# Banks of PSUM in a fused attention and mixer kernel: three for transposes and second products, three for the product groups

## The chip, the cores and the metric

One core of a Trainium2 chip runs the whole program. The metric is the device time of one execution in microseconds (us). Three executions of the kernel before were timed, and one more was taken by the profiler.

## The reference

Attention over 4 batches, 8 heads, 576 positions and head size 64, with a mask: the first four heads see only the last 32 positions (local), the other four only positions of the same residue modulo 32 (strided). Behind it stand two feed-forward blocks in fp32:

```python
scores = np.where(masks[None, :, :, :], scale * np.matmul(q, k.transpose(0, 1, 3, 2)), -1e9)
attn = np.exp(scores - np.max(scores, axis=-1, keepdims=True))
attn = attn / (np.sum(attn, axis=-1, keepdims=True) + 1e-09)
x = np.matmul(attn, v)                              # heads side by side: (4, 576, 512)
h = gelu(x @ w_in); u, v = h[..., :512], h[..., 512:]
v_n = (v - mean(v)) / sqrt(var(v) + 1e-6) * g_ln
v_s = np.einsum('ts,bsd->btd', w_sg, v_n) + b_sg[None, :, None]
x = x + (u * v_s) @ w_out                           # the mixer
xn = (x - mean(x)) / sqrt(var(x) + 1e-6) * g_2
out = x + np.maximum(xn @ w_ch1, 0.0) @ w_ch2       # the last stage
```

## The kernel before, in words

Every fp32 product of the mixer is made of three matmuls on high and low halves (`mm3`, lines 247 to 249). The mixer runs over the four batches, and in each over four segments of product groups: v (five tiles of 128 positions and 512 columns, `v_mm`, lines 598 to 610), u (eight groups of 12 matmuls of 288 columns, `u_group`), g (eight groups of 14, `sg_group`) and y (eight groups of 12, `y_group`). A group fills one bank of PSUM, and the bank is free again when ScalarE (ACT) or VectorE (DVE) has read it: a gelu for v and u (line 354), a product into `z` for g (line 687), an addition into `y` for y (line 717). Of v's fifth tile the two halves are added first (lines 617 and 618). What follows a v tile is `v_norm`: mean and variance on DVE, a power on GpSimd (POOL, line 635), and the scaled tile `vn` on ACT (line 638) and DVE (line 641). Only two buffers `g2` hold the gelus of v, so the gelu of tile t waits for the last reader of tile t - 2. All groups of g need `vn` of all five tiles.

Between the groups stands the attention of the next batch, four pairs of heads, two local (nine blocks of 64 queries) and two strided. A pair has scores (`attn_s`, on PE with masks and maxima on DVE), exponentials (`attn_e`, ACT) and `attn2`: the weights are transposed on PE (`attn_turn`, line 515), copied out of PSUM, multiplied by the values (`attn_values`, lines 542 and 559) and copied into `x32`. In the names, `ps_t` is a bank of transposes, `ps_pv` one of second products, `ps_sc` one of scores.

PSUM has eight banks, in three pools for the whole program:

```python
ps_s = pool("ps_s", 2, space=PSUM)
ps_a = pool("ps_a", 2, space=PSUM)
ps_d = pool("ps_d", 4, space=PSUM)
```

`ps_s` holds scores, `ps_a` transposes and second products, `ps_d` the groups of v, u, g and y. A local pair takes three banks' worth of transposes (four, four and one block) and two of second products (five and four blocks), a strided one two and two.

The start, which is attention of batch 0 and the first four v tiles, runs in an order written out by hand (`START`). These four v tiles are accumulated side by side in the four banks of `ps_d`; the fifth follows when the first has had its gelu. From there on the order on each engine is made by a scheduler out of the program's order and the hooks (`hook(b, segment, group, function)`: called ahead of that group). The hooks of batch 0 at the first u group load the last quarter of `w_in`, and the spatial weights `wsg` are loaded from the fourth u group on (`WSG_AT`), but the scheduler takes both far forward. An engine works its own queue in order. The last stage (`last_stage`) uses all eight banks, and its products are `ps_p` and `ps_m`.

Of the kernel before, what the change touches and what calls it, by code (L numbers as in the profile page):

```python
# [12 lines left out]
F32 = mybir.dt.float32  # L13
# [5 lines left out]
PSUM = bass.MemoryType.PSUM  # L19
# [5 lines left out]
P = 128  # L25
# [160 lines left out]
def mixer_kernel(ctx: ExitStack, tc: tile.TileContext, io, out):  # L186
# [9 lines left out]
    def pool(name, bufs=1, **kw):  # L196
        guard = tc.tile_pool(name=name, bufs=bufs, **kw)
        pools[name] = guard
        return guard.__enter__()

    def close(*names):
        for n in names:
            pools.pop(n).__exit__(None, None, None)
# [4 lines that stand above are left out]
# [284 lines left out]
        attn_sum(b, p)  # L492
        attn_norm(b, p)

    pTs = {}

    def attn_turn(b, p):
        p3 = pend.pop((b, p))[0]
        local = p < NP // 2
        ntr = NLB if local else (NSG + 1) // 2  # L500
        c = P
        pT = pTs[b, p] = at.tile([P, ntr * c], F32, tag=f"pT{local}", name="pT", bufs=1)
        kr = LW if local else P
        for t0 in range(0, ntr, 4):
            m = min(4, ntr - t0)
            ps = ps_a.tile([P, 512], F32, tag="a", name="ps_t")
            rows = kr
            for t in range(t0, t0 + m):
                if local:
                    src = p3[:, t, :]  # L510
                else:
                    e = min(2 * t + 2, NSG)
                    src = pts[p % 2][:, 2 * t * SLOT:e * SLOT]
                    rows = (e - 2 * t) * SLOT
                nc.tensor.transpose(ps[:rows, (t - t0) * c:(t - t0 + 1) * c], src, ident)  # L515

            def copy(r, t, e):
                if t < e:
                    o, i = pT[:r, t * c:e * c], ps[:r, (t - t0) * c:(e - t0) * c]
                    if p in PT_DVE[min(b, 1)]:  # L520
                        nc.vector.tensor_copy(o, i)
                    else:
                        nc.scalar.activation(o, i, AF.Copy)

            copy(kr, t0, t0 + m - (rows < kr))
            if rows < kr:
                copy(rows, t0 + m - 1, t0 + m)

    def attn_values(b, p):
        pT, vt = pTs.pop((b, p)), vts.pop((b, p))  # L530
        local = p < NP // 2
        if p == 0:
            x32s[b] = dw.tile([P, NP, S], F32, tag="x32", name="x32", bufs=2)
            xhls[b] = win.tile([P, 2, NP, SX], F32R, tag="xhl", name="xhl")
        x32 = x32s[b]
        if local:
            for b0 in range(0, NLB, 5):
                m = min(5, NLB - b0)
                ps = ps_a.tile([P, 512], F32, tag="a", name="ps_pv")
                for i in range(b0, b0 + m):  # L540
                    for h in range(2):
                        nc.tensor.matmul(
                            ps[64 * h:64 * h + 64, (i - b0) * QB:(i - b0 + 1) * QB],
                            lhsT=vt[:LW, (i * 2 + h) * D:(i * 2 + h + 1) * D],
                            rhs=pT[:LW, i * P + 64 * (h ^ (i % 2)):i * P + 64 * (h ^ (i % 2)) + QB],
                            start=True, stop=True)
                if p in X32_DVE[min(b, 1)]:
                    nc.vector.tensor_copy(x32[:, p, b0 * QB:(b0 + m) * QB], ps[:, :m * QB])
                else:
                    nc.scalar.activation(x32[:, p, b0 * QB:(b0 + m) * QB], ps[:, :m * QB], AF.Copy)  # L550
        else:
            x3 = x32[:, p, :].rearrange("p (a r) -> p r a", r=STRIDE)
            for o in range(2):
                ps = ps_a.tile([P, 512], F32, tag="a", name="ps_pv")
                ks = slice(64 * o, 64 * o + 64)
                m = (NSG + 1 - o) // 2
                for j in range(m):
                    for h in range(2):
                        nc.tensor.matmul(
                            ps[64 * h:64 * h + 64, j * GW:(j + 1) * GW],  # L560
                            lhsT=vt[ks, (j * 2 + h) * D:(j * 2 + h + 1) * D],
                            rhs=pT[ks, j * P + 64 * (h ^ o):j * P + 64 * (h ^ o) + GW],
                            start=True, stop=True)
                full = m if o else m - 1
                nc.scalar.activation(
                    x32[:, p, :].rearrange("p (a r) -> p a r", r=STRIDE)[:, :, :30]
                    .rearrange("p a (j s) -> p j s a", s=2 * RG)[:, :, o * RG:(o + 1) * RG, :],
                    ps[:, :full * GW].rearrange("p (j r a) -> p j r a", r=RG, a=NPOS), AF.Copy)
                if full < m:
                    r0 = 2 * full * RG  # L570
                    nc.scalar.activation(
                        x3[:, r0:STRIDE, :],
                        ps[:, full * GW:full * GW + (STRIDE - r0) * NPOS].rearrange("p (r a) -> p r a", a=NPOS),
                        AF.Copy)
# [17 lines left out]
    def attn2(b, p):  # L592
        for step in (attn_turn, attn_values, attn_high, attn_low, attn_copy):
            step(b, p)
# [176 lines left out]
    def flush():  # L771
        while late_lows:
            late_lows.pop(0)()
# [42 lines left out]
    def keep(i):  # L816
        nc.sync.dma_start(out=w1_d[i], in_=w1[i].rearrange("p n a f -> p (n a f)").bitcast(F32))
# [44 lines left out]
    def prepare(n):  # L862
        for fn, a in units[done[0]:done[0] + n]:
            if fn is piece and a[1] < 2 and late_lows and wseq.index(a) in PRE:
                flush()
            fn(*a)
        done[0] += n
        if FLUSH:
            flush()
# [557 lines left out]
    def on(fn):  # L1427
        return lambda p: fn(0, p)

    first = {"q": on(attn_load), "m": on(attn_load_v), "K": on(attn_banks), "S": on(attn_scores),  # L1430
             "M": on(attn_max), "E": on(attn_exp), "U": on(attn_sum), "N": on(attn_norm), "T": on(attn_turn),
             "V": on(attn_values), "H": on(attn_high), "L": on(attn_low), "C": on(attn_copy), "w": load_w_v,
             "a": convert_w_v, "b": split_w_v, "v": v_part, "f": fill, "y": fetch_w_u,
             "c": lambda i: load_consts() if i == 0 else nc.sync.dma_start(out=g_v, in_=io["g_v"])}
# [7 lines left out]
    def hook(b, seg, i, fn, *args):  # L1442
        hooks.setdefault((b, seg, i), []).append((fn, args))
# [12 lines left out]
    def right(name, bufs=1):  # L1456
        big[name] = pool("r_" + "_".join(map(str, name)) if isinstance(name, tuple) else name, bufs, side="right",
                         reuse_waits="tile")
        order_r.append(big[name])

    order_r = []

    def open_a():
        close("at")
        right("wst")
        right("nm")
        right("sr")
        right("rb")
        big["norm", 0] = big["nm"].tile([P, KD * TC + 2 * TH], F32, tag="n0", name="n0")
        big["stg"] = big["wst"].tile([P, 3072], U32, tag="stg", name="stg")  # L1470
        big["stg2"] = big["wst"].tile([P, 1792], U32, tag="stg2", name="stg2")
# [13 lines left out]
    def open_d():  # L1485
        close("dn", "dw", "cw")
        for i in (1, 2):
            right(("w2p", i))
        right(("w2", NW - 1))
        right("h")  # L1490
        right("tmp")
        right("ev")
        right("lt")
        right("yc")
        big["late", 0] = big["nm"].tile([P, NLATE, TH], F32, tag="n0", name="late")
        big["late", 1] = big["lt"].tile([P, NF - NLATE, TH], F32, tag="lt", name="late2")

    last = B - 1
    hook(last, "v", 0, open_a)
    hook(last, "g", 0, open_b)  # L1500
    hook(last, "y", 0, open_c)
# [12 lines left out]
    def run(b, seg, n, fn):  # L1514
        for i in range(n):
            for h, args in hooks.get((b, seg, i), ()):
                h(*args)
            fn(b, i)
# [5 lines left out]
    for b, seg in order:  # L1524
        n, fn = segs[seg]
        run(b, seg, n, v_post0 if (b, seg) == (0, "v") else fn)
    open_d()
    prepare(max(0, 13 - done[0]))
    keep(1)
    last_stage()  # L1530
# [17 lines left out]
```

## Time and profile before

| what | us |
|---|---|
| median of the three timed runs | 666.51 |
| the three runs | 666.35, 666.51, 2217.13 |
| the profiled execution | 667.92 |
| its span, first to last instruction | 666.0 |
| PE busy in the span | 648.0 |
| DVE, ACT, POOL busy | 521.7, 397.9, 19.3 |

The profiled execution is 1.9 us longer than its span, and 1.4 us above the median of the timed runs. Matmuls are pipelined: a row's duration runs from issue to a modelled end, so two rows overlap, and the pace is the distance of their starts. A bracket at a row's end is the idle time of the engine ahead of it and what ended it. The mixer takes the first 300 us or so, the last stage the rest.

### The profile page before, as it was taken

To read this page: it belongs to the slowest core of one execution; us is meant where nothing else is said; L and a number is where in the kernel's file an instruction comes from. 1 tells how busy PE (TensorE), PEld (TensorE's weight loads), DVE (VectorE), ACT (ScalarE), POOL (GpSimd) and SP (SyncE) were. 2 spreads that over 40 slices of the span, in tenths; PEclk is the share of its full clock that TensorE was granted. 3 is DMA by queue.
4 is the path that set the end of the run, shared out by engine and by line. 5 is a ranking of instruction groups with operands and counts; after the bars stand their busy time and mean duration, and the time that the engine had idled before them with its cause. 6 is when DMAs were issued, how large, how long until landed. Compare 5 with 4: busy or idle time off the path is not lost.

```text
span 666.0 us, 12893 instructions
## 1 busy us (share of the span) xinstructions
PE 648.0 (97%) x4958; PEld 618.6 (93%) x4958; DVE 521.7 (78%) x997; ACT 397.9 (60%) x908; POOL 19.3 (3%) x24
## 2 busy tenths in 40 slices
PE   8989999999999998999999999999999999999997
PEld 6778989989897988999999999999999999999997
DVE  5979888586668688997799898558474776799993
ACT  4878967284458546645567965357663544766440
POOL 0011011000110001000000000000000000000000
PEclk9999999999999999999999999999999999999999
DMA  7793333458443470429997716499900879522234
GB/s 252 261 299 88 120 108 127 136 168 248 134 140 98 159 224 26 174 96 328 334 348 290 275 56 216 145 324 313 314 5 0 256 244 361 169 78 64 70 101 130
DMA packets 58444, 121.21 MB, mean 182 GB/s; under 512 B 4944, under 2 KB 28112, under 8 KB 57360
## 3 DMA queue, kind: packets, MB, share of 16 engines
q1 hardware_dynamic: 58384, 120.40, 54.2%
q8 instruction: 39, 0.64, 0.4%
q14 instruction: 21, 0.17, 0.1%
HBM read 87.35 MB, written 33.03 MB: 181 GB/s over the span
## 4 chain that ended last, share of the span: by engine, by line
PE 79%; DMA 6%; ACT 6%; DVE 6%; issue 2%; POOL 1%; SPq 0%; ACTq 0%; POOLq 0%; DVEq 0%
PE ps_p L994 26%; PE ps_m L1217 17%; PE ps_o L247 3%; PE ps_o L249 3%; PE ps_o L248 3%; PE ps_y L249 2%; PE ps_y L247 2%; PE ps_y L248 2%; DMA w_scratch<-w_p 2%; PE ps_g L247 2%; PE ps_g L248 2%; PE ps_g L249 2%; DMA stg<-in_w_ch 2%; PE ps_t L515 1%; PE ps_u L247 1%
## 5 line engine op out<-in xcount | busy, mean ns | idle before, releaser
L994 PE MATMUL ps_p<-x,w 128*128 128x384 f32 x1008 | 182.8, 336 | 0.8 <-ACT u L1187 0.5
L994 PEld LDWEIGHTS ps_p<-x,w 128*128 128x128 f32 x1008 | 174.2, 188 | 4.8 <-ACT u L1187 2.0
L1217 PE MATMUL ps_m<-t,w2c 128*128 128x384 f32 x420 | 74.3, 334 | 0.0
L1217 PEld LDWEIGHTS ps_m<-t,w2c 128*128 128x128 f32 x420 | 72.9, 188 | 0.0
L247 PE MATMUL ps_u<-xhl,winl 128*128 128x288 f32 x128 | 38.1, 297 | 1.6 <-ACT u L354 1.6
L247 PE MATMUL ps_g<-wsg,vn 128*128 128x288 f32 x128 | 39.0, 305 | 0.0
L249 PE MATMUL ps_g<-wsg,vn 128*128 128x288 f32 x128 | 38.3, 299 | 0.0
L248 PE MATMUL ps_g<-wsg,vn 128*128 128x288 f32 x128 | 38.1, 297 | 0.0
L249 PE MATMUL ps_y<-gt,wout 128*128 128x288 f32 x128 | 37.8, 296 | 0.0
L249 PE MATMUL ps_u<-xhl,winh 128*128 128x288 f32 x128 | 37.7, 295 | 0.0
L248 PE MATMUL ps_u<-xhl,winh 128*128 128x288 f32 x128 | 37.7, 294 | 0.0
L247 PE MATMUL ps_y<-gt,wout 128*128 128x288 f32 x128 | 37.6, 296 | 0.0
L248 PE MATMUL ps_y<-gt,wout 128*128 128x288 f32 x128 | 37.5, 294 | 0.0
L249 PE MATMUL ps_o<-h,w2x 128*128 128x384 f32 x96 | 32.1, 334 | 0.0
L248 PE MATMUL ps_o<-h,w2x 128*128 128x384 f32 x96 | 32.1, 334 | 0.0
L247 PEld LDWEIGHTS ps_u<-xhl,winl 128*128 128x128 f32 x128 | 24.0, 188 | 2.5 <-ACT u L354 2.1
L635 POOL TENSOR_TENSOR rs<-ve,neghalf 128x1 f32<-128x1 f32 x20 | 19.1, 958 | 242.3 <-DVE ve L633 242.3
L247 PEld LDWEIGHTS ps_g<-wsg,vn 128*128 128x128 f32 x128 | 24.1, 188 | 0.6
L717 DVE TENSOR_TENSOR y<-ps_y,x 128x288 f32<-128x288 f32 x32 | 14.4, 453 | 12.8 <-PE ps_y L249 12.0
L249 PEld LDWEIGHTS ps_g<-wsg,vn 128*128 128x128 f32 x128 | 24.0, 188 | 0.2
L248 PEld LDWEIGHTS ps_g<-wsg,vn 128*128 128x128 f32 x128 | 24.0, 188 | 0.1
L248 PEld LDWEIGHTS ps_u<-xhl,winh 128*128 128x128 f32 x128 | 24.0, 188 | 0.2
(344 smaller groups left out, 1631.3 us busy)
## 6 DMA issues: line engine op xcount, KB each, us to landing
w_scratch<-w SPq DMA_DIRECT2D x8, 1792.0 KB, 7.0
w<-w_scratch SPq DMA_DIRECT2D x24, 512.0 KB, 5.1
stg<-in_w_ch SPq DMA_DIRECT2D x22, 512.0 KB, 5.5
w<-w_scratch SPq DMA_DIRECT2D x36, 256.0 KB, 4.6
raw_p<-in_w_ch SPq DMA_DIRECT2D x20, 256.0 KB, 3.1
blk<-w_scratch SPq DMA_DIRECT2D x10, 512.0 KB, 5.4
qk<-in_qk_s SPq DMA_DIRECT2D x8, 601.0 KB, 4.3
qk<-in_qk_l SPq DMA_DIRECT2D x8, 592.0 KB, 5.0
```

The source lines that it names most:

```text
L247: nc.tensor.matmul(ps, lhsT=ll, rhs=rh, start=first, stop=False)
L248: nc.tensor.matmul(ps, lhsT=lh, rhs=rl, start=False, stop=False)
L249: last_mm[0] = nc.tensor.matmul(ps, lhsT=lh, rhs=rh, start=False, stop=last)
L515: nc.tensor.transpose(ps[:rows, (t - t0) * c:(t - t0 + 1) * c], src, ident)
L635: nc.gpsimd.tensor_tensor(out=rs, in0=ve, in1=neghalf[:, :1], op=ALU.pow)
L717: nc.vector.tensor_tensor(out=y[:, cs], in0=o, in1=x32[:, d, cs], op=ALU.add)
L994: nc.tensor.matmul(o, lhsT=w[:, n0 + nk * k, a, :], rhs=x[:, c, k, :], start=first and k == 0 and n == 0, stop=k == 1 and n == 2, skip_gro ...
L1217: nc.tensor.matmul(banks[e, half][:, :TH], lhsT=sl[m, e][a][:, i, :], rhs=g[:, c, half * TH:(half + 1) * TH], skip_group_check=True, start ...
```

## The change

From the first u group of batch 0 to the last y group of batch 3, the pools are three banks for `ps_a` and three for `ps_d`. Both pools are closed and opened again at that group (a hook), and once more, back to two and four, ahead of the last stage. A tile of a reopened pool waits for what last used its bank. In a local pair the second bank of second products (blocks five to eight) is no tile of its own any more: it lies in columns 128 on of the bank that holds the transpose of the ninth block. This holds for the start too.

```diff
@@ attn_turn
-    pTs = {}
+    pTs, shared = {}, {}
...
             ps = ps_a.tile([P, 512], F32, tag="a", name="ps_t")
+            if local and t0 == 8:
+                shared[b, p] = ps[:, P:]
@@ attn_values
-                ps = ps_a.tile([P, 512], F32, tag="a", name="ps_pv")
+                ps = shared.pop((b, p)) if b0 else ps_a.tile([P, 512], F32, tag="a", name="ps_pv")
@@ behind the hooks of the mixer
+    def banks(a, d):
+        nonlocal ps_a, ps_d
+        close("ps_d", "ps_a")
+        ps_a = pool("ps_a", a, space=PSUM, reuse_waits="tile")
+        ps_d = pool("ps_d", d, space=PSUM, reuse_waits="tile")
+
+    hook(0, "u", 0, banks, 3, 3)
@@ ahead of the last stage
     open_d()
+    banks(2, 4)
```

The scheduler makes another order of it. On ACT, in batch 0 behind the second v tile, stood this before (`u_647<-ps_u_648` is the gelu of the first u group, 662, 688 and 721 are the next three; `g2_601<-ps_v_421` and `g2_614<-ps_v_422` are the gelus of the third and fourth v tile):

```order
L354 ACTIVATE u_647<-ps_u_648 128x288
L354 ACTIVATE g2_601<-ps_v_421 128x512
L218 ACTIVATE wsg_98<-st_104 128x576
L218 ACTIVATE winh_102<-st_104 128x4x128
L638 ACTIVATE vn_101<-g2_588,rs_596 128x512
L354 ACTIVATE u_647<-ps_u_662 128x288
L354 ACTIVATE u_647<-ps_u_688 128x288
L354 ACTIVATE g2_614<-ps_v_422 128x512
L218 ACTIVATE wsg_98<-st_104 128x576
L354 ACTIVATE u_647<-ps_u_721 128x288
```

Now ACT has the following from the fourth v tile's gelu (`g2_612<-ps_v_420`) on; `ps_v_625` is the fifth v tile, and `ps_u_654` and `ps_u_668` are the first two u groups:

```order
L354 ACTIVATE g2_612<-ps_v_420 128x512
L218 ACTIVATE wsg_98<-st_104 128x576
L640 ACTIVATE vn_101<-g2_599,rs_607 128x512
L218 ACTIVATE wsg_98<-st_104 128x576
L619 ACTIVATE g2_634<-ps_v_625 64x512
L640 ACTIVATE vn_101<-g2_612,rs_620 128x512
L354 ACTIVATE g2_634<-g2_634 64x512 x2
L333 ACTIVATE wsg4h_99<-st_104 128x576
L338 ACTIVATE wsg4l_100<-st_104 64x576
L354 ACTIVATE u_653<-ps_u_654 128x288
L640 ACTIVATE vn_101<-g2_634,rs_688 128x512
L354 ACTIVATE u_653<-ps_u_668 128x288
```

The gelu of the first u group stood between those of the second and third v tile; now it stands behind all of v and behind the last two pieces of `wsg`, and the second u group's stands behind the last `vn`. In the built program the first u group waits for the gelu of the fourth v tile, where before it waited for that of the second; the fourth waits for the first group's gelu, and the fifth for the second's.

On SP's queue of transfers, in the same place, stood before (`qk_945` is the third pair's operand for batch 1, the `st` rows on line 328 are rows of `wsg`):

```order
L379 DMA vt_799<-in_v_l 128x1152
L227 DMA raw_o_1265<-in_w_out 128x512
L328 DMA st_104<-in_wsg_t 128x576
L371 DMA qk_945<-in_qk_s 128x1202
L328 DMA st_104<-in_wsg_t 128x576
```

and now:

```order
L379 DMA vt_805<-in_v_l 128x1152
L371 DMA qk_950<-in_qk_s 128x1202
L328 DMA st_104<-in_wsg_t 128x576
L227 DMA raw_o_1269<-in_w_out 128x512
L328 DMA st_104<-in_wsg_t 128x576
```

The transfer of `qk` is ahead of the second row of `wsg` and no longer behind it.

On PE, at the seam of batch 1's g and y, where the second strided pair's transposes stand, before (`ps_t_2194` and `ps_t_2200` are its two banks of transposes, `ps_pv_2163` and `ps_pv_2178` the first strided pair's second products):

```order
L559 MATMUL ps_pv_2163<-pT_2151,vt_1948 64x54 x12
L559 MATMUL ps_pv_2178<-pT_2151,vt_1948 64x54 x10
L247 MATMUL ps_y_2296<-gt_1781,wout_97 128x288
L248 MATMUL ps_y_2296<-gt_1781,wout_97 128x288
L515 MATMUL ps_t_2194<-masks_93,pts1_106 128x128 x4
L515 MATMUL ps_t_2200<-masks_93,pts1_106 128x128
L515 MATMUL ps_t_2200<-masks_93,pts1_106 64x128
```

and now:

```order
L561 MATMUL ps_pv_2165<-pT_2153,vt_1951 64x54 x12
L561 MATMUL ps_pv_2180<-pT_2153,vt_1951 64x54 x10
L517 MATMUL ps_t_2196<-masks_93,pts1_106 128x128 x4
L517 MATMUL ps_t_2202<-masks_93,pts1_106 128x128
L517 MATMUL ps_t_2202<-masks_93,pts1_106 64x128
L247 MATMUL ps_y_2298<-gt_1785,wout_97 128x288
L248 MATMUL ps_y_2298<-gt_1785,wout_97 128x288
```

The transposes follow the second products directly, and the first four go into a third bank. In the last stage no instruction of PE has moved, but for a few of its first products, which now stand among the last y groups of batch 3.

## Rows read from the trace of the kernel before

**Rows 1.** The page, part 1: busy time, share and instructions of each engine
```profile
PE 648.0 (97%) x4958; PEld 618.6 (93%) x4958; DVE 521.7 (78%) x997; ACT 397.9 (60%) x908; POOL 19.3 (3%) x24
```
**Rows 2.** Waits of PE, 0 to 360 us: us in total, times, longest
```profile
PE ps_u L247 <- ACT u L354: 1.6, 2, 1.0
...
PE ps_t L515 <- ACT x L571: 1.3, 2, 0.9
```
**Rows 3.** PE in order of time, batch 0: start, us, instruction, [idle before]
```profile
41.63 0.39 PE L605 MATMUL ps_v<-winl,xhl 128*128 128x512 f32 x1
41.86 0.29 PE L247 MATMUL ps_u<-xhl,winl 128*128 128x288 f32 x1
...
56.94 0.29 PE L249 MATMUL ps_u<-xhl,winh 128*128 128x288 f32 x1
57.07 0.29 PE L247 MATMUL ps_g<-wsg,vn 128*128 128x288 f32 x1
...
60.78 1.30 PE L423 MATMUL ps_sc<-qk 64*64 64x96 f32 x36 [0.77 <-issue]
62.09 0.40 PE L684 MATMUL ps_g<-wsg4l,vn 128*128 128x288 f32 x1
```
**Rows 4.** ACT in order of time, the same stretch
```profile
40.82 0.58 ACT L354 ACTIVATE g<-ps_v 128x512 f32<-128x512 f32 x1
...
49.47 0.60 ACT L354 ACTIVATE g<-ps_v 128x512 f32<-128x512 f32 x1 [0.22 <-DVE vn L641]
...
57.71 0.68 ACT L338 ACTIVATE wsg4l<-st 64x576 fp32r<-64x576 f32 x1
58.41 0.41 ACT L354 ACTIVATE u<-ps_u 128x288 f32<-128x288 f32 x1
60.65 0.72 ACT L638 ACTIVATE vn<-g,rs 128x512 fp32r<-128x512 f32 x1 [1.83 <-POOL rs L635]
...
62.05 1.28 ACT L471 ACT_TABLE_LOAD   x1
```
**Rows 5.** DVE and PE in order of time, batch 0's g: a `z` and a group
```profile
78.00 0.45 DVE L687 TENSOR_TENSOR z<-ps_g,u 128x288 f32<-128x288 f32 x1
...
78.88 0.38 PE L247 MATMUL ps_g<-wsg,vn 128*128 128x288 f32 x1
```
**Rows 6.** DVE and ACT in order of time: readers of v's fifth tile and of u groups
```profile
102.26 0.67 DVE L618 TENSOR_TENSOR g<-ps_v,g 64x512 f32<-64x512 f32 x1
...
191.00 0.39 ACT L354 ACTIVATE u<-ps_u 128x288 f32<-128x288 f32 x1
...
256.38 0.41 ACT L354 ACTIVATE u<-ps_u 128x288 f32<-128x288 f32 x1
```
**Rows 7.** PE in order of time: groups of u in batches 1, 2 and 3
```profile
102.62 0.29 PE L247 MATMUL ps_u<-xhl,winl 128*128 128x288 f32 x1
...
191.03 0.29 PE L247 MATMUL ps_u<-xhl,winl 128*128 128x288 f32 x1
...
254.82 0.29 PE L247 MATMUL ps_u<-xhl,winl 128*128 128x288 f32 x1
...
259.47 0.45 PE L933 MATMUL ps_m<-sr,one 128*128 128x384 f32 x1 [1.31 <-DVE sr L910]
```
**Rows 8.** PE in order of time: transposes of strided pairs in batches 1 and 2
```profile
154.48 0.93 PE L515 MATMUL ps_t<-masks,pts 128*128 128x128 f32 x6 [0.87 <-ACT x L571]
...
223.37 0.66 PE L515 MATMUL ps_t<-masks,pts 128*128 128x128 f32 x4 [0.38 <-ACT x L571]
```
**Rows 9.** PE in order of time, the start: matmuls of 512 columns that only fill
```profile
6.98 3.35 PE L169 MATMUL ps_f<-wout,one 128*128 128x512 f32 x7
...
11.90 2.13 PE L169 MATMUL ps_f<-wout,one 128*128 128x512 f32 x8
```
**Rows 10.** Busy time by stretch: PE, PEld, DVE, ACT, POOL, granted clock, DMA share, GB/s
```profile
0.00:10.00 10.00, 8.18 (x51) 6.22 (x52) 4.60 (x14) 2.66 (x5) 0.20 (x4) 1.00 0.73 245
...
60.00:70.00 10.00, 8.86 (x163) 8.16 (x162) 9.71 (x29) 9.20 (x39) 0.62 (x1) 1.00 0.49 157
```

## The prediction

> **What bounds the kernel now.** I read the page's busy times first: PE works 648.0 of 666.0 us [rows 1], so 18 us of idle time on PE is all that any change of order could give, and whatever holds PE up longer than before is paid in full, unless PE waits for something else later. The waits of PE come next: in the mixer, gelus of u groups hold it for 1.6 us in two places and copies out of second products for 1.3 us in two [rows 2]. Both are waits for a bank. So the question is which bank a group gets, and when its last reader is done. For that I went through PE, ACT and DVE in order of time [rows 3 to 8].
>
> In batch 0 the reader is to see this. The last v matmul starts at 41.63 us, the first u group at 41.86, right behind it [rows 3]: its bank was read by the gelu of the second v tile, done at 40.82 + 0.58 = 41.40 [rows 4]. The gelu of the fourth v tile ends at 49.47 + 0.60 = 50.07 [rows 4]; by then PE has been at u groups for 8 us. All eight end at 57.07, and PE goes on with g before the last tile's `vn` exists: at a pace of 0.13 us (56.94 to 57.07) it starts 21 matmuls of g until 0.77 us ahead of 60.78, then does scores for 1.30 us, and reaches the matmuls that need the last `vn` at 62.09 [rows 3].
>
> **The change part by part.**
>
> *First wait, batch 0's u.* The reopened pool hands out the bank of the fourth v tile first, so no u group starts until 50.07 instead of 41.86. On ACT three gelus of u are gone from ahead of that v gelu, about 1 us, but it waited for `vn` on DVE [rows 4], and the transfer of `qk` is now ahead of a row of `wsg` that ACT copies before it. I take 50.1, between 48.9 and 51. Three groups of 12 x 0.13 = 1.6 us run then, to 54.9.
>
> *Second wait.* The fourth group needs the bank of the first, whose gelu stands behind the copy of `wsg4l`, which ended at 57.71 + 0.68 = 58.39 [rows 4]. One u gelu fewer stands between the last two gelus of v, so I take 58.1, with the gelu of 0.41 us [rows 4] 58.5. The group runs to 60.1.
>
> *Third wait.* The fifth group needs the second's gelu, which stands behind the last `vn`. That one began at 60.65 after 1.83 us of waiting for POOL [rows 4], so it is set by its own chain, not by ACT's load: 0.3 us earlier again, 60.35 + 0.72 + 0.41 = 61.5 (60.6 to 61.8).
>
> *Behind it* four groups and the scores that were moved among them: 4 x 1.6 + 1.30 = 7.7, which is 69.2. Before, the same work stood done at 62.09 less the 21 matmuls of g, 2.7, that is at 59.4. PE is 9.8 us late (8.9 to 10.1). Whether the first wait ends at 49 or 51 does not matter, since the third decides. The early start of g, which had filled the wait for the last `vn`, is gone: that `vn` is now waited for inside u, where nothing stands behind it.
>
> *Batch 0's g with three banks.* A group needs the `z` three groups back, no longer four. Closest is 78.88, with the `z` done at 78.00 + 0.45 = 78.45 [rows 5]: 0.43 us to spare. ACT and DVE are busy 9.20 and 9.71 of 10 us at 60 to 70 [rows 10], and the new order has two more loads of the activation table there, 1.28 us each [rows 4], since the last u gelu now stands between two pairs' exponentials. PE being late hides most of that. 0 to 2.6 us; I take 0.5.
>
> *The u groups of batches 1 to 3.* Batch 1: a group at 102.62 gets the bank of v's fifth tile, free at 102.26 + 0.67 = 102.93: 0.3 us [rows 6, 7]. Batch 2: the group at 191.03 needs the gelu that ends at 191.39, 0.4 us [rows 6, 7]. Batch 3: the group at 254.82 gets the first u group's bank, free at 256.38 + 0.41 = 256.79, so 2.0 us; but PE waited 1.31 us for DVE at 259.47 anyway [rows 6, 7], and that goes into it. I take 0.3, and 1.0 for all three (0.4 to 1.8). In y a read follows its group at once, and three banks suffice; the last y groups of batch 3, whose reads are late, have products of the last stage put between them now. I take 0 for both.
>
> *What is won.* The transposes of strided pairs waited 0.87 and 0.38 us for copies [rows 8]; a third bank takes these waits away, but the fillers that stood before the second products stand behind now, and part of it returns there: -0.9, between -1.25 and 0.
>
> *The shared bank.* The ninth block's transpose and the four last blocks' products read and write the same columns of data as before, and these products had to wait for that copy in any case: 0. Between start and hook the pools are still two and four: 0. A copy and a matmul in one bank at the same time is a thing that the trace before does not show as a cost; bounds by the nearest wait, the smaller of [rows 8], 0 to 0.4 us a batch, of which I take none.
>
> *The sum*: 9.8 + 0.5 + 1.0 - 0.9 = 10.4 us. The profiled execution of 667.92 would be 678.3; on the median of 666.51 it is **676.9**, 1.6% more. A measurement of this kernel tells about 2% from no change, 13.3 us, so this counts as within it.
>
> **Where a rule is weighed.** At the start PE does seven matmuls of 512 columns in 3.35 us, behind pauses, and a little later eight in 2.13 us [rows 9]: 0.48 against 0.27 us each, although the granted clock reads 1.00, its 2.4 GHz level, there as everywhere [rows 10]. The new idle stretch of 8 us has nothing like it in the trace before. The Trainium skill, "TensorE: Matmul & The Clock Gate", Part 1, says that the array falls to 1.2 GHz after it was idle, and returns only after sustained work. By that rule the u groups behind the wait run slowly; the row at the start agrees in pace. By the rows alone, the first three groups can take 2.9 instead of 1.6 us and end at 58.8, where the fourth was to begin at 58.5, and this one still ends ahead of 61.5: a slow pace that ends there is free. What it costs when it lasts is the first rival.
>
> **The rivals.**
>
> *The slow pace lasts through u.* By 0.48 to 0.27, 1.8 times: three groups to 58.8, the fourth to 61.7, four more and the scores 4 x 2.9 + 2.3 = 13.9, to 75.6. That is 16.2 late, with the other terms 16.8: 683.3, slower by more than 2%. For it speaks that PE pauses three times within 20 us, against it that from 50 on no pause is longer than 3.6 us, and that the start reached the fast pace although its fillers were broken up too. It decides from the sixth group on: if that one is still slow, the 2% are passed.
>
> *Only the first wait costs.* If the gelus of u are not held behind `wsg4l` and `vn`, because these come early on an ACT with less to do, the groups run from 50.1 on: 8 x 1.6 + 1.3, to 64.2, 4.8 late, with the rest 5.4: 671.9. For it: ACT has idle time there. Against: `vn` waited for POOL, not for ACT [rows 4].
>
> *Not slower at all.* PE had to wait for the last `vn` until 62 us before too, so the idle time might only have moved, and the third bank's 1.25 us remain: 665.3. That needs v's gelus some 8 us earlier, against two buffers for them and the chain over DVE and POOL; and PE did useful work for 15 us there.
>
> *ACT and DVE fall behind in batch 0's g.* If the two table loads come through to the `z` reads, 2.6 in place of 0.5, and each later bank wait takes its upper bound, 1.8 for 1.0 with nothing won: 9.8 + 2.6 + 1.8 = 14.2, 680.7. Against it: PE, late itself, gives both engines time.
>
> **How the numbers follow.** Forecast 0.58, the slow pace 0.14, only the first wait 0.16, not slower 0.04, ACT and DVE behind 0.08. The forecast's own bounds are 8.9 + 0 + 0.4 - 1.25 and 10.1 + 1.5 + 1.8, so 674.6 to 679.9. The range goes down to 671.5, which takes in the case of the first wait, and up to 682.5, into a slow pace that ends before the last group: it leaves out about 0.18. Faster by over 2% would need 13 of PE's 18 idle us: 0.02 for what I have not seen. Slower by over 2%: 0.14, half of the last rival, and a tail of the forecast, 0.20. Within 2%: 0.78.
>
> **What would show it.** In the profile after, PE waits for the gelu of a v tile between about 42 and 50 us, for u's gelu until about 58.5 and again until 61.5; the eighth u group ends near 69, and g's first group runs through without a break. ACT shows three table loads around batch 0's exponentials. The u waits of batches 1 to 3 read `ps_u` <- ACT or DVE, under 2 us each; no `ps_t` <- ACT `x` of 0.87 near batch 1's end. From the mixer's end on, every row lies about 10 us later at an unchanged pace. I am wrong if the first u group starts well before 48 us, if v's gelus come earlier than 47, or if rows of 288 columns follow each other at 0.24 us and not 0.13 beyond 62 us.

## The result, and the profile after

Six executions of the changed kernel took 674.73 to 677.65 us, median 676.03; the kernel before, beside it, 666.43. The ratio is 1.015, with a 95% interval of 1.0128 to 1.0172: 9.6 us slower (8.5 to 11.5 by the interval), clear of no difference but within the bound of 2%. Single executions of 2217.13 us here, and of 2695.86 and 1615.28 us in the experiments, are counted in the medians and left out of the ratios. The forecast was 676.9 us. The profiled execution took 676.43, its span is 674.6.

The page's totals hardly show it: PE's busy time grew by 1.1 us against [rows 1], its idle time by 7.5.

```profile
PE 649.1 (96%) x4958; PEld 619.2 (92%) x4958; DVE 522.6 (77%) x997; ACT 401.1 (59%) x910; POOL 19.5 (3%) x24
```

The waits of PE from 0 to 360 us (us in total, times, longest), which answer to [rows 2]:

```profile
PE ps_u L247 <- ACT g L354: 7.8, 1, 7.8
PE ps_u L247 <- ACT u L354: 3.9, 4, 1.8
```

Two u waits of together 1.6 us became five of 11.7, and behind the start no wait of `ps_t` for ACT's `x` is left. PE in order of time in batch 0 (start, us, instruction, idle before), answering to [rows 3]:

```profile
39.85 0.40 PE L607 MATMUL ps_v<-winl,xhl 128*128 128x512 f32 x1
...
48.36 0.61 PE L247 MATMUL ps_u<-xhl,winl 128*128 128x288 f32 x1 [7.80 <-ACT g L354]
...
51.40 0.44 PE L247 MATMUL ps_u<-xhl,winl 128*128 128x288 f32 x1
...
53.19 0.29 PE L247 MATMUL ps_u<-xhl,winl 128*128 128x288 f32 x1
...
56.73 0.41 PE L247 MATMUL ps_u<-xhl,winl 128*128 128x288 f32 x1 [1.79 <-ACT u L354]
...
59.57 0.40 PE L247 MATMUL ps_u<-xhl,winl 128*128 128x288 f32 x1 [0.98 <-ACT u L354]
...
62.95 1.04 PE L423 MATMUL ps_sc<-qk 64*64 64x96 f32 x36
...
67.20 0.29 PE L247 MATMUL ps_g<-wsg,vn 128*128 128x288 f32 x1
```

The three waits are those of the forecast, and g then runs through. The start, whose order did not change, was 1.78 us earlier in this execution (last v matmul at 39.85, before at 41.63), so 1.78 is to be added where times of the two traces are compared. ACT in the same stretch, answering to [rows 4]:

```profile
47.71 0.60 ACT L354 ACTIVATE g<-ps_v 128x512 f32<-128x512 f32 x1 [0.31 <-DVE mv L633]
...
55.56 0.68 ACT L338 ACTIVATE wsg4l<-st 64x576 fp32r<-64x576 f32 x1
56.26 0.41 ACT L354 ACTIVATE u<-ps_u 128x288 f32<-128x288 f32 x1
58.50 0.72 ACT L640 ACTIVATE vn<-g,rs 128x512 fp32r<-128x512 f32 x1 [1.83 <-POOL rs L637]
59.13 0.39 ACT L354 ACTIVATE u<-ps_u 128x288 f32<-128x288 f32 x1
```

The first u gelu stands behind `wsg4l`, the second behind the last `vn`, which again waited 1.83 us for POOL. Busy time by stretch (PE, PEld, DVE, ACT, POOL, granted clock, DMA share, GB/s), answering to [rows 10]:

```profile
40.00:50.00 10.00, 2.20 (x11) 1.83 (x10) 9.04 (x19) 6.66 (x11) 3.42 (x3) 0.75 0.75 247
50.00:60.00 10.00, 7.23 (x46) 6.77 (x46) 9.34 (x19) 6.66 (x13) 1.91 (x2) 0.91 0.21 63
60.00:70.00 10.00, 10.00 (x142) 9.50 (x140) 4.19 (x13) 5.62 (x21) 0.00 (x0) 1.00 0.18 63
```

The granted clock, 1.00 up to the wait, its 2.4 GHz level, fell in it: read from 48.4 to 51.4 us it is 0.50, the 1.2 GHz level. The first u group took 3.04 us (48.36 to 51.40), the second 1.79, later ones 1.6.

PE's waits in the u groups of batches 1 and 2, and the `sr` wait of batch 3, answering to [rows 7]:

```profile
118.32 0.40 PE L247 MATMUL ps_u<-xhl,winl 128*128 128x288 f32 x1 [0.93 <-ACT u L354]
...
194.07 0.40 PE L247 MATMUL ps_u<-xhl,winl 128*128 128x288 f32 x1 [0.22 <-ACT u L354]
...
267.09 0.44 PE L935 MATMUL ps_m<-sr,one 128*128 128x384 f32 x1 [0.19 <-DVE sr L912]
```

Read at the first matmuls of stages, the changed kernel is 8.21 us late at batch 1's u (107.65 against 99.44) and 7.61 at the last stage's first `ps_o` (314.15 against 306.54). With the 1.78 us of the start these are 9.99 and 9.39: all of the price is paid in batch 0.

### The profile page after: what moved, and what is told of

It is laid out like the page before. It is cut to its first block, busy times and chain, and to the rows that moved or that the text cites. A ratio compares the mean times of both kernels' runs of the same rounds, so it can differ in the third digit from the quotient of the medians.

```text
span 674.6 us, 12901 instructions
## 1 busy us (share of the span) xinstructions
PE 649.1 (96%) x4958; PEld 619.2 (92%) x4958; DVE 522.6 (77%) x997; ACT 401.1 (59%) x910; POOL 19.5 (3%) x24
## 4 chain that ended last, share of the span: by engine, by line
PE 64%; DVE 11%; ACT 10%; DMA 9%; issue 2%; POOL 2%; SPq 0%; POOLq 0%; ACTq 0%; DVEq 0%
PE ps_p L996 20%; PE ps_m L1219 17%; PE ps_o L247 3%; PE ps_o L249 3%; PE ps_o L248 3%; DMA stg<-in_w_ch 3%; PE ps_y L249 2%; PE ps_y L247 2%; PE ps_y L248 2%; ACT pt L471 2%; DMA w_scratch<-w_p 2%; POOL rs L637 2%; PE ps_g L247 1%; ACT vn L640 1%; DVE vn L643 1%
## 5 line engine op out<-in xcount | busy, mean ns | idle before, releaser
L247 PE MATMUL ps_u<-xhl,winl 128*128 128x288 f32 x128 | 39.5, 309 | 11.8 <-ACT g L354 7.8
L248 PEld LDWEIGHTS ps_u<-xhl,winh 128*128 128x128 f32 x128 | 24.7, 193 | 0.1
L247 PEld LDWEIGHTS ps_g<-wsg,vn 128*128 128x128 f32 x128 | 24.0, 188 | 0.7
L249 PEld LDWEIGHTS ps_u<-xhl,winh 128*128 128x128 f32 x128 | 24.7, 193 | 0.0
L248 PEld LDWEIGHTS ps_g<-wsg,vn 128*128 128x128 f32 x128 | 24.0, 188 | 0.3
```

Of the source, the lines that this page charges most:

```text
L247: nc.tensor.matmul(ps, lhsT=ll, rhs=rh, start=first, stop=False)
L248: nc.tensor.matmul(ps, lhsT=lh, rhs=rl, start=False, stop=False)
L249: last_mm[0] = nc.tensor.matmul(ps, lhsT=lh, rhs=rh, start=False, stop=last)
```

## The experiments

Two theories stood at the outset. *The reopening*: closing the pools while v tiles are still unread puts the gelus of u behind all of v on ACT, and the u groups that wait for them are late. *The banks*: u, g and y lack a fourth bank. Two more came up inside the first: that the 7.8 us ahead of the first group (the wrong bank handed out first) are the price, and that the slow pace behind it is.

**Reopened as three and three, but a batch later**

```diff
-    hook(0, "u", 0, banks, 3, 3)
+    hook(1, "v", 0, banks, 3, 3)
```

> The pools are closed and reopened as three and three one segment of a batch later, ahead of the first v group of batch 1; batch 0's u and g have two and four as before, and the rest of the change stands. Theory (the loss is batch 0's u, where the reopened pool hands out the bank of the fourth v tile): the first u group starts right behind the last v matmul near 42 us, the wait of 7.8 us for the gelu of v and the two of 1.79 and 0.98 for gelus of u are gone, and what is left of the change is the sum of the later differences, about 1 us: 667 to 668 us. Rival (three banks cost the groups throughout, by waits in u, g and y of every batch): 674 to 676 us, with waits of ps_u, ps_g or ps_y that add up to 8 us in batches 1 to 3.

Measured: 665.93 us, ratio 1.0009 (0.999 to 1.0029). PE in batch 0:

```profile
40.81 0.40 PE L607 MATMUL ps_v<-winl,xhl 128*128 128x512 f32 x1
41.05 0.29 PE L247 MATMUL ps_u<-xhl,winl 128*128 128x288 f32 x1
...
60.55 1.29 PE L423 MATMUL ps_sc<-qk 64*64 64x96 f32 x36 [0.75 <-issue]
```

The time is below the theory's 667 to 668 us: three banks from batch 1 on make no difference on balance. In this trace u of batches 1 and 2 takes 0.7 and 1.0 us longer than in the trace before (14.40 and 14.78 us), and the stretches from the last u of batches 1 and 2 to the next batch's first are 0.7 and 0.9 us shorter (67.56 and 55.20). The whole loss goes with the place of the hook.

**The shared bank alone**

```diff
-    hook(0, "u", 0, banks, 3, 3)
...
-    banks(2, 4)
```

> Only the shared bank is left of the change: the pools stay two and four for the whole program and are never reopened. Theory (the shared bank costs nothing, since the four last blocks' products waited for the copy of the ninth block's transpose in any case): 666.4 us, 665.7 to 667.1, and no wait for ps_pv that was not there before. Rival (a copy and matmuls in one bank hold each other up, 0.4 us for each local pair, eight of them): 668 to 670 us.

Measured: 665.92 us, ratio 1.0013 (0.9986 to 1.0041). The interval ends at +2.7 us and so does not reach the middle of the rival, 3.2 us. For the second products of local pairs PE waited 0.9 us here and 0.8 before, one wait each; a wait of 0.4 us at a strided pair, which has no shared bank, is new.

**Reopened in the same place, with two and four banks**

```diff
-    hook(0, "u", 0, banks, 3, 3)
+    hook(0, "u", 0, banks, 2, 4)
...
-    banks(2, 4)
```

> Both pools are closed and reopened at the same place, ahead of batch 0's first u group, but as two and four again; with four banks for the groups and the shared bank. Theory (what costs is that a reopened pool hands out its banks in its own order, and no longer the one that is free): in the built program the first u group gets the bank of the fifth v tile and waits for its readout, so PE waits 8 us or more behind the last v matmul, the next three groups follow without a wait, and the time is 674 to 679 us. Rival (what costs is the fourth bank that u lacks): the first u group starts near 42 us and the time is 666 to 668 us.

Measured: 677.34 us, ratio 1.0185 (1.0145 to 1.0224). PE:

```profile
41.23 0.39 PE L607 MATMUL ps_v<-winl,xhl 128*128 128x512 f32 x1
41.55 0.38 PE L423 MATMUL ps_sc<-qk 64*64 64x96 f32 x2
54.10 0.61 PE L247 MATMUL ps_u<-xhl,winl 128*128 128x288 f32 x1 [12.17 <-DVE g L620]
```

Reopening alone, with every bank that the kernel before has, costs the whole price. The banks as a theory fall. The built program before says the same in another way: its eight u groups of batch 0 use only three banks, since the fourth holds v's fifth tile. But another wait sets the price here: the first group gets the bank of v's fifth tile, and no u group behind it waits for a bank, so the 12.17 us are not covered by anything later. A reopening can cost by the bank that it hands out first, too.

**Skip the first bank**

```diff
+    def skip():
+        t = ps_d.tile([P, 512], F32, tag="d", name="ps_skip")
+        nc.vector.memset(t[:, :8], 0.0)
+
+    hook(0, "u", 0, skip)
```

> The changed kernel, but at the reopening one more tile takes the first bank that the pool of groups hands out (the fourth v tile's) and DVE writes 8 columns of zeros to it, so the first u group gets the bank of the second v tile, which is free. In the built program the first two u groups wait only for the gelus of the second and third v tile, the third for DVE's write, and the fourth for the first group's gelu, which now stands behind the last vn on ACT. Theory (only the last wait decides, the one for a gelu behind the last vn; the 7.8 us ahead of the first group are covered by it): the 7.8 us wait is gone, the first group starts right behind the last v matmul, the fourth starts about 59.6 us, where the fifth started before, one group later than in the changed kernel: 676 + 1.5 = 677.5 us (676.5 to 678.5). Rival (the first wait is what costs, 6.5 us of it beside the kernel before): 669 to 670.5 us.

Measured: 678.26 us, ratio 1.0162 (1.0115 to 1.021). PE:

```profile
40.08 0.40 PE L247 MATMUL ps_u<-xhl,winl 128*128 128x288 f32 x1
...
43.95 0.40 PE L247 MATMUL ps_u<-xhl,winl 128*128 128x288 f32 x1 [2.02 <-ACT g L354]
...
54.32 0.58 PE L247 MATMUL ps_u<-xhl,winl 128*128 128x288 f32 x1 [8.52 <-DVE ps_skip L1474]
...
59.23 0.61 PE L247 MATMUL ps_u<-xhl,winl 128*128 128x288 f32 x1 [1.70 <-ACT u L354]
...
62.28 0.44 PE L247 MATMUL ps_u<-xhl,winl 128*128 128x288 f32 x1
```

The first group starts 8 us earlier than in the changed kernel and nothing is won. The 8.52 us are the experiment's own, for DVE's write; they end 4.9 us ahead of the group that needs the first gelu, at 59.23, and that one still has to wait. In the changed kernel the largest wait of the profile is worth nothing by itself, since a later one covers it. Here the slow pace does cost: it falls behind the last wait, where the fourth group took 3.05 us (59.23 to 62.28) and the fifth 2.17 (to 64.45), 2.0 us more than two groups of 1.6.

**Only the gelus moved**

```diff
+    put_off, last_vn, last_sg = [], [None], [None]
+
+    def late_gelus():
+        for op in (last_sg[0], last_vn[0], last_vn[0], last_vn[0]):
+            gelu(*put_off.pop(0))
+            tc.add_manual_dep(last_gelu[0].ins, op.ins.name, ORDER, reason="behind")
...
-        gelu(us[b][:, f, cs], ps[:, :SH])
+        if b == 0 and i < 4:
+            put_off.append((us[b][:, f, cs], ps[:, :SH]))
+        else:
+            gelu(us[b][:, f, cs], ps[:, :SH])
...
+    hook(0, "u", 4, late_gelus)
```

`last_sg` is the copy of `wsg4l`, `last_vn` the last `vn`; the pools are never reopened.

> No pool is reopened and the pools stay two and four (the shared bank remains); only the gelus of batch 0's first four u groups are put off on ACT, the first behind the copy of wsg4l, the other three behind the last vn, the places that they have in the changed kernel. Theory (the price of the change is the order of these gelus on ACT and nothing else of the reopening): the first u group starts right behind the last v matmul, as before; the fifth waits for the first one's gelu and the sixth for the second's, behind the last vn, so three groups and the scores stand behind it where in the changed kernel four groups did: 676 - 1.6 = 674.4 us (673.3 to 675.5). Rival (the price is the bank that a reopened pool hands out, or its third bank against four): 666 to 667.5 us.

Measured: 675.0 us, ratio 1.0135 (1.0087 to 1.0184). PE and, behind it, ACT:

```profile
55.94 0.40 PE L247 MATMUL ps_u<-xhl,winl 128*128 128x288 f32 x1 [1.66 <-DVE g L626]
...
59.40 0.40 PE L247 MATMUL ps_u<-xhl,winl 128*128 128x288 f32 x1 [1.60 <-ACT u L354]
...
62.24 0.40 PE L247 MATMUL ps_u<-xhl,winl 128*128 128x288 f32 x1 [0.26 <-ACT u L354]
```
```profile
58.93 0.41 ACT L354 ACTIVATE u<-ps_u 128x288 f32<-128x288 f32 x1
61.17 0.72 ACT L646 ACTIVATE vn<-g,rs 128x512 fp32r<-128x512 f32 x1 [1.83 <-POOL rs L643]
61.80 0.39 ACT L354 ACTIVATE u<-ps_u 128x288 f32<-128x288 f32 x1
```

With the pools of before, and only four gelus in the places that the reopening gave them, the price is there: 0.9 to 1.8% by the interval, the change's was 1.3 to 1.7. That rests on three executions, 674.73 to 675.12 us. From the last v matmul to the last stage's first `ps_o` PE is 7.3 us later than in the trace before, in the changed kernel 9.4; the 2.1 us between them are near the 1.6 of the one group less that stands behind the last `vn`. The places of these gelus are enough to cause the price of the change.

**Reopened in the middle of u**

```diff
-    hook(0, "u", 0, banks, 3, 3)
+    hook(0, "u", 4, banks, 3, 3)
```

> The pools are reopened as three and three in the middle of batch 0's u, ahead of its fifth group. The first four groups and their gelus stand as in the kernel before; the gelu of the fifth stands behind the copy of wsg4l, and the eighth group waits for it. Theory (a reopening costs what is queued behind the release of all the old tiles, so half of u costs less than half): the first u group starts right behind the last v matmul, the eighth starts near 58.5 instead of 55.5 us, g starts with the last vn near 62 us, and the 21 matmuls of g that ran ahead of it are lost, 2.7 us: 669 to 670 us. Rival (any reopening inside u brings the whole price): 674 us or more.

Measured: 673.39 us, ratio 1.0104 (1.007 to 1.0137): between the two numbers, so both missed. PE:

```profile
51.61 0.29 PE L247 MATMUL ps_u<-xhl,winl 128*128 128x288 f32 x1
...
59.63 1.96 PE L423 MATMUL ps_sc<-qk 64*64 64x96 f32 x36 [6.26 <-issue]
...
61.52 0.61 PE L247 MATMUL ps_u<-xhl,winl 128*128 128x288 f32 x1
...
64.56 0.40 PE L247 MATMUL ps_u<-xhl,winl 128*128 128x288 f32 x1
```

I had looked at the u groups alone. In the new order 36 scores stand ahead of the seventh group, and they waited 6.26 us; DVE's additions of masks, which read the scores' banks, stood behind v's normalization and began at 58.97. The seventh group then ran at the slow pace (3.04 us). Half of u seems to cost less than the whole (the interval just overlaps the change's, 1.0128 to 1.0172); how much less is set by what else is queued.

**Reopened ahead of g**

```diff
-    hook(0, "u", 0, banks, 3, 3)
+    hook(0, "g", 0, banks, 3, 3)
```

> The pools are reopened as three and three ahead of batch 0's first g group, so that u stands as in the kernel before and g of batch 0 has three banks. In the built program the first two g groups wait for the gelus of the sixth and seventh u group, which are early. Theory (three banks are enough for g, and the whole loss is u's reopening): the waits around 60 us are those of the kernel before and the time is 666 to 667 us. Rival (g with three banks costs what the forecast's upper bound said, 2.6 us, or a reopened pool stalls wherever it stands): 668.5 to 670 us, with waits of ps_g for ACT or DVE.

Measured: 668.56 us, ratio 1.0032 (1.0009 to 1.0055). No wait of `ps_g` for ACT or DVE stands in its trace. Longer than before is the wait ahead of the scores, 1.41 against 0.77 us in [rows 3]:

```profile
60.38 1.29 PE L423 MATMUL ps_sc<-qk 64*64 64x96 f32 x36 [1.41 <-issue]
```

Ahead of that wait PE had started 15 matmuls of g, before 21 [rows 3]; the first matmul that needs the last `vn` follows it at the same distance in both traces (1.44 and 1.43 us behind the start of that `vn` on ACT), so six matmuls more, 0.8 us, stand behind it. By its time the run stands at the rival, by its waits at the theory, and its interval overlaps that of the batch-later hook. What three banks in batch 0's g cost when PE is not late stays open between 0.6 and 3.7 us.

**Fill the first wait**

```diff
+    def warm():
+        ps = ps_a.tile([P, 512], F32, tag="a", name="ps_w")
+        for n in range(28):
+            op = nc.tensor.matmul(ps, lhsT=one, rhs=wout[:, 0, 0, :], start=True, stop=True, skip_group_check=True)
+            if n == 0:
+                tc.add_manual_dep(op.ins, last_mm[0].ins.name, ORDER, reason="behind v")
+
+    hook(0, "u", 0, warm)
```

> The changed kernel with 28 matmuls of 512 columns put behind the fifth v tile, whose product nothing uses: PE is busy in the 7.8 us in which it waited for the gelu of the fourth v tile. Theory (the slow pace of 0.24 us a matmul in the first four u groups behind that wait is free, since the fifth group has to wait for a gelu that stands behind the last vn): the granted clock reads 1.00 from 40 to 60 us, the u groups go at 0.13 us from the first on, the waits for gelus of u grow by what the pace gives back, the fifth u group starts within 0.5 us of where it did, and the time is that of the changed kernel, 675 to 677 us. Rival (the slow pace is part of the price): the fifth group starts 1.5 to 3 us earlier and the time is 673 to 674.5 us.

Measured: 678.9 us, ratio 1.0217 (1.0176 to 1.0259), outside both. PE, then ACT:

```profile
40.20 6.69 PE L1474 MATMUL ps_w<-wout,one 128*128 128x512 f32 x28
46.82 0.38 PE L423 MATMUL ps_sc<-qk 64*64 64x96 f32 x2
51.02 0.40 PE L247 MATMUL ps_u<-xhl,winl 128*128 128x288 f32 x1 [3.82 <-ACT g L354]
```
```profile
44.25 0.69 ACT L218 ACTIVATE wsg<-st 128x576 fp32r<-128x576 f32 x1 [3.25 <-DMA st<-in_wsg_t]
...
50.37 0.60 ACT L354 ACTIVATE g<-ps_v 128x512 f32<-128x512 f32 x1 [0.88 <-DVE mv L633]
...
61.75 0.73 ACT L640 ACTIVATE vn<-g,rs 128x512 fp32r<-128x512 f32 x1 [2.13 <-POOL rs L637]
```

The fill moved other work: ACT waited 3.25 us for a row of `wsg` that it had copied at 41.59 in the changed kernel, and the last `vn` came at 61.75 instead of 58.50. The time grew by 2.9 us with it. Nor was the slow pace gone: the granted clock reads 0.83 from 50 to 60 us. So this run does not separate the slow pace from the wait, as it was meant to; it agrees with a time that goes with the last `vn`.

**Three and three beside g and y only**

```diff
-    hook(0, "u", 0, banks, 3, 3)
+    for b in range(1, B - 1):
+        hook(b, "g", 0, banks, 3, 3)
+        hook(b + 1, "v", 0, banks, 2, 4)
```

> Three and three only where the strided transposes had waited: from the first g group of batches 1 and 2 to the first v group of the next batch; two and four elsewhere. Theory (the third bank takes away waits of 0.87 and 0.38 us for copies of second products, and u keeps its fourth bank): 665.2 to 666.2 us, no wait of ps_t for ACT's x in batches 1 and 2. Rival (what the third bank takes away comes back at other waits, and each of the four reopenings costs a few tenths): 666.4 to 668 us.

Measured: 668.62 us, ratio 1.003 (1.0005 to 1.0055). This lies above both expectations. The waits of `ps_t` for ACT's `x` are gone, as the theory has it, but waits of scores for DVE have grown, as the rival has it. The first line is of this run, the second of the kernel before (PE from 0 to 360 us):

```profile
PE ps_sc L423 <- DVE pt L445: 2.1, 2, 1.5
```
```profile
PE ps_sc L423 <- DVE pt L445: 0.3, 1, 0.3
```

The profiled execution was the fastest of the twelve, 665.7 us, so its trace does not show what made the median 2.9 us longer. No version beat the kernel before.

## Why the prediction was right

*First wait.* Forecast: first u group at 50.1, 8.5 us behind the last v matmul. Measured: 48.36 - 39.85 = 8.5.

*Second and third wait.* Forecast 58.5 and 61.5, less the 1.78 of the start 56.7 and 59.7. Measured 56.73 and 59.57. That the third decides, and the first does not, is what the run with the skipped bank shows.

*Behind it.* Forecast: the scores and groups done at 69.2, less 1.78 67.4, 9.8 late. Measured 67.20, so 9.6. The early start of g is gone, as written; it had hidden the wait for the last `vn`.

*Batch 0's g.* Forecast 0.5. Measured 0.4: from g's first matmul, 9.6 late, to batch 1's u, 9.99. It is not a wait for a `z`, which the forecast had: no wait of `ps_g` stands in the trace; transposes and second products wait there, 0.34, 0.25 and 0.25 us.

*The u groups of batches 1 to 3.* Forecast 0.3, 0.4 and 0.3, together 1.0. Measured from the first to the last u matmul of a batch: 14.99 against 13.75 us, 14.53 against 13.74 and 15.19 against 16.32, that is +1.24, +0.79 and -1.13, together 0.9. The sum is right by chance, and the places were wrong. In batch 1 not the third group waits, 0.3 us, but the seventh, 0.93, for the fourth one's gelu (ACT does it from 117.88 to 118.27). In batch 2 it is chiefly the third, 0.22, and not the seventh. In batch 3 the first gelu came 2.9 us behind the start of its group and no longer 5.1, so the expected wait of 2.0 us did not arise, and the wait of `ps_m` for `sr` fell from 1.31 to 0.19 us, which I had only set against the loss. The losses repeat: with three banks batch 1's u takes 14.40 to 15.41 us in six traces, with four 13.74 to 13.75 in five.

*Won at the transposes.* Forecast -0.9, at most -1.25. Measured from the last u of one batch to the first u of the next: 67.87 against 68.30 and 54.99 against 56.07, -1.51. The term was sized too small by 0.6, the largest miss. The second stretch repeats: 54.99 to 55.28 us in five traces with three banks there (56.32 in the run with the fill, 57.42 in the one reopened beside g and y), 55.92 to 56.07 in four with two and four.

*Together.* The terms measured make 9.4 in place of 10.4 us; the medians differ by 9.6.

*Shared bank.* Forecast 0; the run with it alone is not told from no change.

*The slow pace.* The granted clock read 0.75 and 0.91, three groups took 6.57 us (48.36 to 54.93) where the fast pace makes 4.8 and the slow one 8.7, and it ended ahead of the second wait, so that 1.79 us of waiting were left: free in this trace, as the working has it. No run tests it by itself. The Trainium skill, "TensorE: Matmul & The Clock Gate", Part 1, which lets the clock fall in an idle stretch and come back under sustained work, agrees with this trace. The rival that let the pace last through u fell, but in the run with the skipped bank its mechanism is seen, at 2.0 us.

*The rivals.* "Only the first wait costs" fell by the second and third wait. "Not slower" fell in batch 0. ACT and DVE did not fall behind in g.

What the prediction did not have, and no run shows, is why the scheduler puts the gelus there. It read their new places and priced them; that these are enough for the price, with no pool reopened, came out of the run with only the gelus moved.

## What to carry to other kernels

A tile of a pool that is closed and reopened in the middle of work waits for the last reader of the bank that it is handed, which need not be the bank that is free, and in the runs here that reopened inside batch 0's u the scheduler also put readers of the new tiles far back. Do it at a seam where no bank is waited for, as here ahead of batch 1's v, where no cost was seen (1.0009, 0.999 to 1.0029). The longest wait in a profile need not be the price: ask which wait decides, and move only the readers to test it. Price a late bank by what stands behind the last of its waits.

## What was not expected of the hardware

The same seven fill matmuls of the start took 3.35 us in the trace before [rows 9] and this in that of after:

```profile
6.97 2.10 PE L169 MATMUL ps_f<-wout,one 128*128 128x512 f32 x7
...
10.44 2.14 PE L169 MATMUL ps_f<-wout,one 128*128 128x512 f32 x8
```

The granted clock reads 1.00 over these 10 us in both, though the pace differs. In the run with the shared bank alone they took 1.90 us. The next row began 1.46 us earlier in the trace after (10.44 against 11.90), most of the 1.78 us by which its start was ahead. The last v matmul lies anywhere from 39.06 to 42.30 us in the eleven traces, and the last stage, hardly changed on PE, took 357.6 to 360.5 us from its first `ps_o` to the span's end in the same eleven. Single traces must be compared stage by stage. The same page of the Trainium skill, in the same part, says that the number of slow matmuls differs from run to run of one kernel, and these rows agree.

The slow pace also came late: in the run with the fill, PE stood idle from 47.2 to 51.02 us, did its first eight u matmuls within 1.18 us, and then 14 at 0.24 us each, from 52.20 to 55.55. The granted clock reads 1.00 over the pause, and 0.50, the 1.2 GHz level, from 52.2 to 55.5. Here a pause of 3.82 us was paid for after the work had begun again.
